# The output projection's weights in other parts, and one part in five transfers of unequal height

## Chip, cores and metric

One core of a Trainium2 chip runs the whole program. The metric is the device time of one execution in microseconds (us). The kernel before took 187.05 us, the median of three runs (187.05 to 187.24).

## What is computed

One decode step (a single new token for each of two batch rows) of a transformer block with adaptive layer norm: attention against a cache, then a gated FFN. Cut to what matters:

```python
mod = (silu(c) @ w_mod).reshape(2, 6, 1, -1)          # sa, ca, ga, sb, cb, gb
h = layernorm(x) * (1 + ca) + sa
q = (h @ wq) -> 32 heads of 192; k, v = the last 1024 rows of the caches
o = softmax(q k^T * 192**-0.5) v                       # per batch row and head
x = x + ga * (o.reshape(2, 1, 6144) @ wo)              # wo: 6144 x 640
h = layernorm(x) * (1 + cb) + sb
x = x + gb * ((gelu(h @ w_gate) * (h @ w_up)) @ w_down)
```

All inputs are bf16. With two rows of x, each weight and each cache row is read once and used little: the program moves some 77 MB for a few matmuls.

## The kernel before

The program is a list of operations per engine, written out in order. A helper class adds an operation or a DMA to its engine's list and derives from named buffers which semaphores it waits for. All DMAs are issued by SP in one order, through line 341, and so stand in one queue that 16 DMA engines work off.

That order is: w_mod, c, x, wq, four loads of K (two tiles each), five of V, then wo in parts, w_gate, w_up, and w_down in three parts, at the end the output. Two large areas of SBUF hold them: a ring of four tiles for K, V and at last the FFN's weights, and one area (`r1`) for wq, later K and V tiles, then wo (`wo_v`).

A load of a weight takes all 128 partitions: partition p gets rows p*n to p*n + n - 1 of the matrix, one contiguous stretch of memory. For wo that is 48 rows of 640 values per partition, and `WO_SPLIT` (line 227) cuts the 48 into parts that are loaded by a DMA each, with a semaphore each (`sem_wo`), lines 679 to 683. They wait for the last two uses of V of batch row 0 (`keep["pv", 0, 2]` and `keep["pv", 0, 3]`), whose area they overwrite. w_gate, w_up and w_down wait for the first uses of V of batch row 1.

```python
        for i, (ta, tb) in enumerate(wo_of):
            S.dma("sp", k_dma(wo_v[:, ta:tb, :].rearrange("p t n -> p (t n)"), wo_src[:, ta:tb, :].rearrange("p t n -> p (t n)")),
                  sem_wo[i], writes=[("wo", i)], deps=[keep["pv", 0, t] for t in (NTL - 2, NTL - 1)], name="ld_wo%d" % i)
```

Stages: the modulation and first layer norm, q (line 491), the scores as products on DVE (line 529) that PE sums (line 548), the softmax (from line 568), the weighted sum of V (lines 590 and 602), the output projection (line 706, one PE operation for each part of wo, which waits for that part), the second layer norm (line 716), the FFN (line 724 for w_gate and w_up, line 747 for w_down), and the two DVE operations and the store at the end (lines 754 to 758). Between the steps of the projection and of the FFN, PE runs matmuls whose results nobody reads (`warm`, line 521; how many is in `WO_WARM`, `WU_WARM`, `WD_WARM`).

Of the kernel before, what the change touches and what calls it, by code (L numbers as in the profile page):

```python
# [172 lines left out]
def bass_adaLN_cond__sliding_block_cached__geglu_ffn__decode_kernel(  # L173
# [15 lines left out]
    P = 128  # L189
# [18 lines left out]
    NTL = KP // J  # L208
# [15 lines left out]
    SL = J * Dh  # L224
    WQ_SPLIT = [5]
    assert sum(WQ_SPLIT) == KT
    WO_SPLIT = [16, 16, 12, 4]
    OT_SPLIT = [16, 16, 16]
    assert sum(WO_SPLIT) == NT and sum(OT_SPLIT) == NT
    WU_SPLIT = [5]  # L230
# [10 lines left out]
    with es:  # L241
        S = _Sched(nc, es)
# [6 lines left out]
        wo_v = r1.rearrange("p (t n) -> p t n", t=NT)  # L249
# [3 lines left out]
        def aux_f(a, n):  # L253
            assert a + n <= NAUX
            return aux[:, a:a + n]
# [18 lines left out]
        oT = aux_f(RN, NT * SQ).rearrange("p (t m) -> p t m", m=SQ)  # L274
# [48 lines left out]
        BK_M = 0  # L323
        SC = 256

        def bank(k):
            return ("bank", k)
# [4 lines left out]
        sem_wq = [S.sem("d_wq%d" % i) for i in range(len(WQ_SPLIT))]  # L332
        sem_wo = [S.sem("d_wo%d" % i) for i in range(len(WO_SPLIT))]
        sem_wg = S.sem("d_wg")
# [5 lines left out]
        def k_dma(dst, src):  # L340
            return lambda e: e.dma_start(dst, src)  # L341
# [5 lines left out]
        def dram_rows(v):  # L347
# [9 lines left out]
             reads=[("S", 0, 0, 0), ("S", 0, 0, 1), ("S", 0, 1, 0), ("S", 0, 1, 1)], writes=["ident_f"], name="ident_f")  # L357
        S.op("pool", lambda e: e.tensor_copy(out=ident_b[:, :], in_=ident_f[:, :]),
             reads=["ident_f"], writes=["ident_b"], name="ident_b")
# [3 lines left out]
             reads=["ident_f"], writes=["G32"], name="G32")  # L363
        S.op("dve", lambda e: e.tensor_reduce(out=M32[:, :], in_=ident_f[:, :].rearrange("p (h t) -> p h t", t=QP), axis=AX.X, op=ALU.add),
             reads=["ident_f"], writes=["M32"], name="M32")
# [3 lines left out]
             reads=["G32"], writes=["Bsel"], name="Bsel")  # L369
# [3 lines left out]
             reads=["M32"], writes=["DS"], name="DS")  # L373


        for b in range(2):
            S.op("dve", (lambda b: lambda e: e.tensor_copy(
                out=SEL[:, b, :, BS * b:P:SQ], in_=G32[:, :].rearrange("p (j m) -> p m j", m=HM)))(b),
                reads=["G32"], writes=["SEL"], name="SEL%d" % b)
        for b in range(2):  # L380
            for m in range(HM):
# [3 lines left out]
                    reads=["ident_f"], writes=["Qsel"], name="Qsel%d%d" % (b, m))  # L385
# [7 lines left out]
        keep = {}  # L393
# [14 lines left out]
        def slot_of(*it):  # L408
            return place[it]
# [75 lines left out]
        for i, (ka, kb) in enumerate(wq_of):  # L485
            def f(e, ka=ka, kb=kb):
                last = None
                for k in range(ka, kb):
                    for c in range(NQC):
                        for j in range(NJ):  # L490
                            last = e.matmul(ps[SQ * j:SQ * j + SQ, BK_H + c, 0:QC], lhsT=hT[:, k, :],  # L491
                                            rhs=wq_v[:, k, RN * j + QC * c:RN * j + QC * (c + 1)],
                                            start=(k == 0), stop=(k == KT - 1), tile_position=(0, SQ * j), skip_group_check=True)
                return last
# [22 lines left out]
        def warm(n, bk):  # L517
            def f(e):
                last = None
                for _ in range(n):  # L520
                    last = e.matmul(ps[:, bk, 0:2 * Dh], lhsT=ident_b[:, :], rhs=qbc[:, :, :].rearrange("p b d -> p (b d)"),  # L521
                                    start=True, stop=True)
                return last
            if n:
                S.op("pe", f, reads=["ident_b", "qbc"], writes=[bank(bk)], name="warm")
# [148 lines left out]
        for i, nt in enumerate(OT_SPLIT):  # L674
            S.op("dve", (lambda t0, nt: lambda e: e.transpose(oT[:, t0:t0 + nt, :], oc.rearrange("p (q k) -> p k q", k=NT)[:, t0:t0 + nt, :]))(t0, nt),  # L675
                 reads=[("oc", c) for c in range(NQC)], writes=[("oT", t) for t in range(t0, t0 + nt)], name="oT%d" % i)
            t0 += nt

        wo_src = A_wo.rearrange("(p t) n -> p t n", t=NT)
        wo_of = [(sum(WO_SPLIT[:i]), sum(WO_SPLIT[:i + 1])) for i in range(len(WO_SPLIT))]  # L680
        for i, (ta, tb) in enumerate(wo_of):
            S.dma("sp", k_dma(wo_v[:, ta:tb, :].rearrange("p t n -> p (t n)"), wo_src[:, ta:tb, :].rearrange("p t n -> p (t n)")),
                  sem_wo[i], writes=[("wo", i)], deps=[keep["pv", 0, t] for t in (NTL - 2, NTL - 1)], name="ld_wo%d" % i)
        assert slot_of("v", 1, 0) == 0 and slot_of("v", 1, 1) == 1
        r3_dead = [keep["pv", 1, 0], keep["pv", 1, 1]]
        S.dma("sp", k_dma(wg_v.rearrange("p k n -> p (k n)"), B_w_gate.rearrange("(p k) n -> p (k n)", k=KT)), sem_wg,
              writes=["wg"], deps=r3_dead, name="ld_wg")
# [13 lines left out]
        for i, (ta, tb) in enumerate(wo_of):  # L701
            def f(e, ta=ta, tb=tb):
                last = None
                for t in range(ta, tb):
                    for j in range(NJ):
                        last = e.matmul(ps[SQ * j:SQ * j + SQ, BK_M, 0:DN], lhsT=oT[:, t, :], rhs=wo_v[:, t, DN * j:DN * j + DN],  # L706
                                        start=(t == 0), stop=(t == NT - 1), tile_position=(0, SQ * j), skip_group_check=True)
                return last
            S.op("pe", f, reads=[("wo", i)] + [("oT", t) for t in range(ta, tb)], writes=[bank(BK_M)], name="wo%d" % i)
            warm(WO_WARM[i], 1)  # L710

        S.op("dve", lambda e: e.tensor_tensor(out=lnt[:, 0, :], in0=ps[:, BK_M, 0:DN], in1=modC[:, 2, :], op=ALU.mult),  # L712
             reads=[bank(BK_M), ("modC", 0)], writes=[("lnt", 0)], name="ga_attn")
        S.op("dve", lambda e: e.tensor_tensor(out=X2[:, 0, :], in0=lnt[:, 0, :], in1=X2[:, 0, :], op=ALU.add),
             reads=[("lnt", 0)], writes=[("X2", 0)], name="x1")
# [3 lines left out]
        def ffn_gu(bk, wv, key, name, ka, kb):  # L719
            def f(e):  # L720
# [11 lines left out]
             reads=[bank(BK_G[0])], writes=["gl"], name="gelu")  # L732
        k0 = 0
        for ci, nk in enumerate(WU_SPLIT):
# [4 lines left out]
             reads=[bank(BK_G[1]), "gl"], writes=["aC"], name="geglu")  # L739
        to_contraction(aT[:, :, :], aC[:, :], FT, ["aC"], ["aT"], "aT")  # L740
        f0 = 0
        for ci, nf in enumerate(WD_SPLIT):
            def f(e, f0=f0, nf=nf):
# [11 lines left out]
             reads=[bank(BK_C), ("modC", 1)], writes=[("lnt", 1)], name="gb_y")  # L755
        S.op("dve", lambda e: e.tensor_tensor(out=sc[:, :], in0=lnt[:, 1, :], in1=X2[:, 0, :], op=ALU.add),
             reads=[("lnt", 1), ("X2", 0)], writes=["sc"], name="outC")
# [36 lines left out]
```

## Time and profile before

| What | us |
|---|---|
| median of three runs | 187.05 |
| the profiled execution | 187.73 |
| its span, first to last instruction | 186.5 |
| busy: PE 117.4, DVE 106.6, ACT 13.9, POOL 4.9 | |
| DMA: 76.99 MB at 413 GB/s on the mean | |
| wo's four parts issued by SP | 138.42 to 140.18 |
| wo's parts landed | 156.83, 162.94, 168.22, 169.79 |
| w_gate, w_up landed | 174.37, 178.96 |
| w_down's three parts landed | 181.29, 182.82, 183.61 |

The profile counts from the start of the span. A DMA has landed when its semaphore has its last increment; the trace keeps the time of every increment and, for each packet on a DMA engine, its start, length and size, though not the engine's number. A 128-row load of wo appears as 128 packets of one row each and 16 packets of 4 bytes that raise the semaphore. PE is TensorE's matmuls, PEld its weight loads, DVE is VectorE, ACT ScalarE, POOL GpSimd, and SPq the DMA issues of SyncE.

### The profile page before, as it was taken

Reading aid. Unit: us, or ns where it says so; the run is one execution under the profiler, and the core shown is the slowest. Engines: PE = TensorE matmul, PEld = TensorE weight load, DVE = VectorE, ACT = ScalarE, POOL = GpSimd, SP = SyncE. Lnnn points to the kernel's source line nnn. Section 1 sums busy time; section 2 is a strip of 40 time slices with the busy share of each in tenths; the row PEclk is TensorE's granted clock in tenths of the full one; section 3 lists DMA queues with packets and bytes.
Section 4 is the critical chain, followed back from the end, with each engine's and each line's share of the span. In section 5 each row is a group of like instructions: output and inputs, shape, how many; then the busy total and the mean of one; then the engine's idle time right before and its main releaser. Section 6 shows DMA issues by size and latency. Waiting matters only on the chain.

```text
span 186.5 us, 2487 instructions
## 1 busy us (share of the span) xinstructions
PE 117.4 (63%) x1014; PEld 61.6 (33%) x1014; DVE 106.6 (57%) x114; ACT 13.9 (7%) x24; POOL 4.9 (3%) x12
## 2 busy tenths in 40 slices
PE   0004500860079998898988987329964998359854
PEld 0001200540034443444334443125642665236422
DVE  6801600020584999999999994454919453903431
ACT  2001400022000000000000000110010003200400
POOL 8100000000000000000000000000000000000000
PEclk9999999997557999999999999855998799996999
DMA  7999999899998989999998999999899999999980
GB/s 264 395 462 488 448 435 398 358 499 401 443 464 380 485 371 485 411 432 453 401 474 369 496 401 443 453 401 446 364 438 432 427 423 426 415 421 435 412 346 20
DMA packets 2923, 76.99 MB, mean 413 GB/s; under 512 B 356, under 2 KB 356, under 8 KB 868
## 3 DMA queue, kind: packets, MB, share of 16 engines
q1 hardware_dynamic: 2916, 76.88, 96.4%
q8 instruction: 6, 0.10, 0.2%
q14 instruction: 1, 0.01, 0.0%
HBM read 76.88 MB, written 0.00 MB: 412 GB/s over the span
## 4 chain that ended last, share of the span: by engine, by line
DMA 42%; DVE 36%; PE 17%; SPq 1%; ACT 1%; issue 1%; POOL 1%; DVEq 0%; POOLq 0%
DVE store L529 26%; DMA store<-in_A_k_cache_dram 24%; DMA store<-in_B_w_down_dram 17%; PE ps L602 11%; DVE Sg L562 5%; PE ps L548 4%; DVE Em L590 2%; SPq L341 1%; PE ps L541 1%; ACT E_sb L581 1%; PE ps L583 1%; PE ps L577 1%; DVE On L619 0%; ACT On L615 0%; PE ps L570 0%
## 5 line engine op out<-in xcount | busy, mean ns | idle before, releaser
L529 DVE TENSOR_TENSOR store<-store,qbc 128x6144 bf16<-128x6144 bf16 x16 | 53.5, 3347 | 8.8 <-DMA store<-in_A_k_cache_dram 8.8
L548 PE MATMUL ps<-store,ident_b 128*128 x192 | 46.5, 394 | 6.2 <-DVE store L529 6.2
L548 PEld LDWEIGHTS ps<-store,ident_b 128*128 128x128 bf16 x192 | 19.3, 100 | 31.4 <-issue 14.7
L602 PE MATMUL ps<-store,Em 128*64 128x384 bf16 x256 | 25.0, 364 | 6.6 <-DVE Em L590 6.6
L590 DVE TENSOR_TENSOR Em<-E_sb,M32b 128x2048 bf16<-128x2048 bf16 x8 | 18.1, 2288 | 5.9 <-PE ps L602 5.9
L602 PEld LDWEIGHTS ps<-store,Em 128*64 128x64 bf16 x256 | 15.7, 123 | 15.6 <-DVE Em L590 7.7
L541 PE MATMUL ps<-qbc,ident_b 128*128 128x384 bf16 x64 | 13.6, 338 | 10.9 <-DVE store L529 10.9
L468 PE MATMUL ps<-store,scT 128*32 128x480 bf16 x40 | 4.4, 601 | 15.8 <-DVE scT L425 15.8
L562 DVE TENSOR_REDUCE Sg<-ps 128x32 f32<-128x512 f32 x16 | 10.9, 683 | 5.7 <-PE ps L548 5.7
L491 PE MATMUL ps<-store,hT 128*32 128x384 bf16 x80 | 5.7, 470 | 10.7 <-DMA store<-in_A_wq_dram 10.7
L541 PEld LDWEIGHTS ps<-qbc,ident_b 128*128 128x128 bf16 x64 | 6.3, 100 | 17.0 <-issue 11.6
L501 DVE CAST aux<-ps 128x384 bf16<-128x384 f32 x4 | 2.0, 552 | 16.5 <-PE ps L491 15.6
L521 PE MATMUL ps<-qbc,ident_b 128*128 128x384 bf16 x56 | 11.0, 338 | 0.0
L706 PE MATMUL ps<-store,aux 128*32 128x160 bf16 x192 | 5.1, 269 | 5.2 <-issue 2.1
L491 PEld LDWEIGHTS ps<-store,hT 128*32 128x32 bf16 x80 | 3.2, 136 | 13.7 <-issue 11.6
L468 PEld LDWEIGHTS ps<-store,scT 128*32 128x32 bf16 x40 | 1.2, 132 | 17.3 <-DVE scT L425 15.8
L581 ACT ACTIVATE E_sb<-Sg,nb 128x256 bf16<-128x256 f32 x2 | 1.0, 508 | 78.0 <-DVE nb L580 78.0
L521 PEld LDWEIGHTS ps<-qbc,ident_b 128*128 128x128 bf16 x56 | 5.2, 101 | 3.8 <-issue 1.1
L706 PEld LDWEIGHTS ps<-store,aux 128*32 128x32 bf16 x192 | 4.2, 111 | 6.7 <-issue 4.4
L619 DVE TENSOR_SCALAR On<-ps,rden 32x192 bf16<-32x192 f32 x4 | 1.7, 418 | 7.6 <-ACT On L615 7.6
L712 DVE TENSOR_TENSOR lnt<-ps,modC 128x160 f32<-128x160 f32 x1 | 0.3, 325 | 7.8 <-PE ps L706 7.8
L675 DVE STREAM_TRANSPOSE aux<-aux 128x512 bf16<-128x512 bf16 x3 | 4.1, 1430 | 0.1
(70 smaller groups left out, 57.2 us busy)
## 6 DMA issues: line engine op xcount, KB each, us to landing
store<-in_A_k_cache_dram SPq DMA_DIRECT2D x4, 6144.0 KB, 39.7
store<-in_A_v_cache_dram SPq DMA_DIRECT2D x3, 6144.0 KB, 20.8
store<-in_A_wq_dram SPq DMA_DIRECT2D x1, 7680.0 KB, 30.5
store<-in_A_v_cache_dram SPq DMA_DIRECT2D x2, 3072.0 KB, 15.0
store<-in_A_wo_dram SPq DMA_DIRECT2D x2, 2560.0 KB, 21.3
store<-in_w_mod_dram SPq DMA_DIRECT2D x1, 4800.0 KB, 14.1
store<-in_A_wo_dram SPq DMA_DIRECT2D x1, 1920.0 KB, 28.9
store<-in_B_w_gate_dram SPq DMA_DIRECT2D x1, 1920.0 KB, 24.7
```

What stands on the lines that cost most here:

```text
L468: last = e.matmul(ps[SQ * j:SQ * j + SQ, bk, 0:3 * DN].rearrange("p (i n) -> p i n", i=3), lhsT=scT[:, k, :], rhs=wm_v[:, k, 3 * part * D: ...
L491: last = e.matmul(ps[SQ * j:SQ * j + SQ, BK_H + c, 0:QC], lhsT=hT[:, k, :], rhs=wq_v[:, k, RN * j + QC * c:RN * j + QC * (c + 1)], start=( ...
L521: last = e.matmul(ps[:, bk, 0:2 * Dh], lhsT=ident_b[:, :], rhs=qbc[:, :, :].rearrange("p b d -> p (b d)"), start=True, stop=True)
L529: S.op("dve", lambda e: e.tensor_tensor(out=tile_v(ks)[:, hf * JH:(hf + 1) * JH, :], in0=tile_v(ks)[:, hf * JH:(hf + 1) * JH, :], in1=qbc[ ...
L541: last = e.matmul(ps[:, BK_W, 0:2 * Dh], lhsT=ident_b[:, :], rhs=qbc[:, :, :].rearrange("p b d -> p (b d)"), start=True, stop=True)
L548: last = e.matmul(o_ap, lhsT=ident_b[:, :], rhs=tile[:, hf * JH:(hf + 1) * JH, ci * GC:(ci + 1) * GC], start=(ci == 0), stop=(ci == NCH - 1))
L562: S.op("dve", lambda e: e.tensor_reduce(out=S_sb[:, b, a:a + JH], in_=ps[:, hf, 0:JH * GC].rearrange("p (j c) -> p j c", j=JH), axis=AX.X, ...
L581: S.op("act", lambda e: e.activation(out=E_sb[:, b, :], in_=S_sb[:, b, :], func=ACTF.Exp, scale=SCALE, bias=nb[:, 0:1], accum_out=esum[:, ...
L590: S.op("dve", lambda e: e.tensor_tensor(out=Em[:, t % 2, :, :], in0=E_sb[:, b, J * t:J * (t + 1)].unsqueeze(2).broadcast_to([P, J, H]), in ...
L602: last = e.matmul(ps[r:r + 2 * H, BK_O, 0:ON], lhsT=Em[:, t % 2, 2 * jp:2 * jp + 2, :].rearrange("p j c -> p (j c)"), rhs=tile_v(vs)[:, 2 ...
L675: S.op("dve", (lambda t0, nt: lambda e: e.transpose(oT[:, t0:t0 + nt, :], oc.rearrange("p (q k) -> p k q", k=NT)[:, t0:t0 + nt, :]))(t0, n ...
L706: last = e.matmul(ps[SQ * j:SQ * j + SQ, BK_M, 0:DN], lhsT=oT[:, t, :], rhs=wo_v[:, t, DN * j:DN * j + DN], start=(t == 0), stop=(t == NT ...
```

## The change

wo's 48 rows per partition are cut 16, 16, 10, 6 instead of 16, 16, 12, 4. The third part goes out as five DMAs instead of one, one after another on SP: partitions 0 to 111, then 112 to 116, 117 to 121, 122 to 124 and 125 to 127. All five raise the semaphore of the third part, by 16 each, and the projection's third operation waits for all of them. What lands where in SBUF, the matmuls and their order stay the same, except that 40 of them instead of 48 belong to the third operation and 24 instead of 16 to the fourth.

```diff
-    WO_SPLIT = [16, 16, 12, 4]
+    WO_SPLIT = [16, 16, 10, 6]
+    UNEVEN = 2
+    EVEN_ROWS = 112
+    FEW = [5, 5, 3, 3]
+    assert EVEN_ROWS + sum(FEW) == P
...
+        wo_keys = []
         for i, (ta, tb) in enumerate(wo_of):
-            S.dma("sp", k_dma(wo_v[:, ta:tb, :].rearrange("p t n -> p (t n)"), wo_src[:, ta:tb, :].rearrange("p t n -> p (t n)")),
-                  sem_wo[i], writes=[("wo", i)], deps=[keep["pv", 0, t] for t in (NTL - 2, NTL - 1)], name="ld_wo%d" % i)
+            dst, src = wo_v[:, ta:tb, :].rearrange("p t n -> p (t n)"), wo_src[:, ta:tb, :].rearrange("p t n -> p (t n)")
+            pieces = [(dst, src)]
+            if i == UNEVEN:
+                pieces, p0 = [(dst[0:EVEN_ROWS, :], src[0:EVEN_ROWS, :])], EVEN_ROWS
+                for n in FEW:
+                    pieces.append((dst[p0:p0 + n, :], src[p0:p0 + n, :]))
+                    p0 += n
+            for k, (to, frm) in enumerate(pieces):
+                S.dma("sp", k_dma(to, frm), sem_wo[i], writes=[("wo", i, k)],
+                      deps=[keep["pv", 0, t] for t in (NTL - 2, NTL - 1)], name="ld_wo%d_%d" % (i, k))
+            wo_keys.append([("wo", i, k) for k in range(len(pieces))])
...
-            S.op("pe", f, reads=[("wo", i)] + [("oT", t) for t in range(ta, tb)], writes=[bank(BK_M)], name="wo%d" % i)
+            S.op("pe", f, reads=wo_keys[i] + [("oT", t) for t in range(ta, tb)], writes=[bank(BK_M)], name="wo%d" % i)
```

## The prediction

> **What bounds the kernel now.** I read the page's slices first, then the chain that ended last in order of time, then the end of the span in short stretches, and last the trace's records of single DMA packets. The page:
>
> ```profile
> span 186.5 us, 2487 instructions
> DMA  7999999899998989999998999999899999999980
> q1 hardware_dynamic: 2916, 76.88, 96.4%
> q8 instruction: 6, 0.10, 0.2%
> q14 instruction: 1, 0.01, 0.0%
> ```
>
> The 16 DMA engines are busy in every slice up to the last two, while no compute engine is. The second to last line shows six packets that fetch instructions on the same DMA engines; they matter below. The chain, in order of time (start, length, what):
>
> ```profile
> 151.47 32.13 DMA store<-in_B_w_down_dram
> 183.61 0.04 issue
> 183.65 0.35 PE ps L747 x8
> 184.00 0.02 issue
> 184.03 0.34 DVE lnt L754
> 184.37 0.02 issue
> 184.39 0.32 DVE sc L756
> ```
>
> The last piece of w_down was issued at 151.47, landed at 183.61, and 2.9 us of tail follow. So the end moves one for one with that landing, as long as PE is ready for it. Busy times by stretch (columns: window, length, busy time of PE, its weight loads, DVE, ACT, POOL, then clock, DMA share, GB/s):
>
> ```profile
> 178.00:180.00 2.00, 0.99 (x21) 0.51 (x22) 0.00 (x0) 0.00 (x0) 0.00 (x0) 1.00 1.00 406
> 180.50:181.00 0.50, 0.42 (x3) 0.03 (x1) 0.47 (x2) 0.00 (x0) 0.00 (x0) 1.00 0.74 292
> 181.00:181.50 0.50, 0.00 (x0) 0.00 (x0) 0.50 (x1) 0.00 (x0) 0.00 (x0) 1.00 0.44 179
> 182.00:182.50 0.50, 0.50 (x18) 0.24 (x8) 0.00 (x0) 0.00 (x0) 0.00 (x0) 1.00 0.22 87
> 183.00:183.50 0.50, 0.50 (x17) 0.26 (x16) 0.00 (x0) 0.00 (x0) 0.00 (x0) 1.00 0.01 5
> ```
>
> The share falls from 1.00 to 0.01 over 3 us: the 16 engines don't finish together. The packet records say why. On one DMA engine each packet starts within some ns of the end of the one before, and all run the same sequence of sizes (8 rows of every 128-row load, then a 4-byte packet), so the records chain into 16 sequences. Their last packets end at 180.40, 180.54, 180.56, 180.64, 180.74, 180.93, 181.00, 181.18, 181.20, 181.72, 182.13, 182.15, 182.17, 182.54, 182.66 and 183.18. The last six are the six whose sequence holds a 16,384-byte fetch (941 to 1102 ns, at 39.3, 130.1, 147.0, 163.9, 170.7 and 179.1 us); the one at 181.72 holds the 8,192-byte fetch at 66.7. A fetch sets its engine back by about 1.45 us against the median engine, for good. So one DMA engine bounds the kernel, 2.2 us behind the median one.
>
> **The change, part by part.** Prices first. Start to start on one engine, a row of 15,360 bytes takes 0.573 us, of 7,680 0.289, of 5,120 0.193. All lie on one line, 26.9 GB/s, so a row of the new third part (10 x 1,280 = 12,800 bytes) takes 0.289 + 5,120/7,680 x (0.573 - 0.289) = 0.478.
>
> Who gets which rows: 128-row loads raise their semaphore 16 times as they land, eight rows to an engine. The loads of c and x, whose outer size is 4, raise it four times, on the same four engines, those that end at 180.40, 180.93, 181.20 and 181.72. I take it that 112 rows go to 16 engines, seven each, and that 5 rows go to five and 3 rows to three engines of one fixed order, the four of c and x being its first. Call them engines 0 to 3; which is which the trace doesn't say, nor which engine is 4.
>
> Per engine, third and fourth part: before 8 x 0.573 + 8 x 0.193 = 6.13 us. After, engines 5 to 15: 7 x 0.478 + 8 x 0.289 = 5.66, a gain of 0.47. Engines 3 and 4 carry two rows more: + 0.49. Engines 0 to 2 carry four more: + 1.44, and four more 4-byte packets of some 13 ns, + 0.05. By this alone the last engine ends at 183.18 - 0.47 = 182.71, if engine 4 is none of the late ones and the one of 181.72 is engine 3 (181.20 + 1.49 = 182.69 for the latest of 0 to 2).
>
> What this leaves out is where the bytes go. The trace has no row for several DMA engines that write into neighbouring partitions at once. Bounds: nothing, if the pace of 26.9 GB/s is the engine's own; or, if it is that of the place written to, rows of one small transfer pass one behind the other. In full, all 16 rows in a file: 7.65 us instead of 4 x 0.478 = 1.91, + 5.74. One observation decides for me: the pace is the same in the full stream and for the last engine alone at 183 us (2,560 bytes in 99 ns both times), so it isn't shared bandwidth but something private, and in every load of 128 rows every engine has eight partitions to itself. The change is the first to break this pairing. An engine's own limit would look the same; I give the place 6 chances in 10. Sixteen places for 128 partitions hold eight each, so rows 112 to 119 and 120 to 127 lie behind two. The transfers of 5, 5, 3 and 3 rows then cost engines 0 to 2 at worst 5 + 3 + 3 + 3 = 14 rows of 0.478, 6.69, which is 4.78 over the free price. The four known engines reach the place up to 1.3 us apart (they ended that far apart), and engines that don't meet don't queue: I take half, 0.6, off. So engines 0 to 2 lose 1.44 + 4.78 - 0.6 = 5.6 us, from about 181.1 (the middle of the four) to 186.7: + 3.5 on 183.18. The place's usual engine shares it too and loses at most eight rows, 3.8 us, less its 0.47, hence no more than these. The seven rows per engine of the 112-row transfer might lose the pairing as well: nothing, or a doubling, 7 x 0.478 = 3.3; I take nothing, since each engine still has a run of its own.
>
> [...]
>
> Smaller edits. Four more issues on SP: 432 ns each by the wo rows, 547 to 716 by those of x and c, 1.7 to 2.9 us in all:
>
> ```profile
> 138.42 1.76 SPq L341 DMA_DIRECT2D store<-in_A_wo_dram  x4
> 149.67 0.33 SPq L341 DMA_DIRECT2D store<-in_B_w_gate_dram  x1
> ```
>
> Only wo's last part stands behind them; its first packet moves at 165. SP's next issue waits for PE until 149.67, so nine us are free and I cost this at nothing; without that cover, up to 2.9. PE waits once for wo part 2 as before, now for five landings. Its last wo step has 24 matmuls instead of 16: 64 take 1.29 us, so + 0.13 us on the way to the FFN. That is hidden by the wait for w_up:
>
> ```profile
> 179.00 1.00 PE L724 MATMUL ps<-store,hT 128*32 128x384 bf16 x20 [1.38 <-DMA store<-in_B_w_up_dram]
> 183.06 0.26 PEld L747 LDWEIGHTS ps<-store,aux 128*32 128x32 bf16 x16 [0.32 <-DMA store<-in_B_w_down_dram]
> ```
>
> In the slow case wo's last part lands on engines 0 to 2 at about 167.2 + 5.6 + 0.6 + 0.4 = 173.8 (median end of that part, loss, lag, landing) instead of 169.79, and the way to w_up's matmuls, 7 us of DVE and PE from there, ends near 181; w_up itself lands at 176.5 + 6.6 = 183.1. So DMA still ends last and the tail of 2.9 us stays.
>
> Sum: + 3.5 us. The profiled span is 186.5 inside an execution of 187.73; the median of the unprofiled runs is 187.05. I add the difference to that: 190.5, with 189.0 to 192.0 as the range of this case (loss 4.1 to 7.1 instead of 5.6).
>
> **Rivals.** First, the engine's own pace: writes to neighbours cost nothing, the last engine gains 0.47 us, PE follows (w_up lands 0.47 earlier, and PE's 0.32 us of idle before the w_down matmuls shows that it keeps up): 186.6. For it: the line through all row sizes needs no second limit. Against it: it needs both engine 4 and the one of 181.72 to be in the right place. Second, free writes but the wrong engines: with the one of 181.72 among engines 0 to 2 it ends at 181.72 + 1.49 = 183.21, no change, 187.1; with a late one as engine 4, the 183.18 one at worst, + 0.49, 187.5. [...]
>
> [...]
>
> **How the numbers follow.** Queue at the place 0.57, gain 0.25, about even 0.10, engine 4 late 0.04, one engine or a 112-row transfer that queues too 0.04. Some 0.2% (0.37 us) is what a measurement of this kernel can tell from no change. Faster is the gain case, 0.26 with a stray share of the even one; same 0.10; slower the rest, 0.64. The likeliest is slower: 190.5. The range runs from the gain, 186.5, to 192.2; what is left out is the queue beyond 5.1 us and the third rival.
>
> **What would show it.** Right: in the after trace wo part 2 lands over 2 us later than at 168.22, packets of 12,800 bytes on few engines take two to five times 0.478 us while the others keep pace, and three engines end last. Wrong: rows of 12,800 bytes keep 0.478 us everywhere, the DMA share falls to zero within 2.5 us instead of 3, and the last landing comes at 183.1. Were a fetch to hit one of engines 0 to 4 in the new program, 1.45 us would be added there, and the sum would fail in the gain case.

## The result and the profile after

The changed kernel takes 192.8 us, the median of six runs (192.56 to 193.29), against 187.05 (186.97 to 187.24): 1.031 times as long, 95% interval 1.0293 to 1.0327, or 5.75 us more. The forecast was 190.5, with 186.5 to 192.2 as the range: the right way, three fifths of the size, and the time lies 0.6 us outside.

The page of the changed kernel (a slice is 4.79 us):

```profile
span 191.6 us, 2491 instructions
DMA  7999998998999989989989999899999999999991
GB/s 248 417 554 410 423 410 369 482 465 359 482 400 431 474 359 482 472 349 492 451 369 472 441 400 472 369 475 400 405 426 451 417 410 346 213 195 427 426 380 41
q1 hardware_dynamic: 2932, 76.88, 96.7%
q8 instruction: 6, 0.10, 0.2%
q14 instruction: 1, 0.01, 0.0%
```

Slices 34 to 36, from 158 to 172 us, are where the time goes: 346, 213 and 195 GB/s, where the kernel before had more than 400. The row of DMA shares shows 9 all the same: the engines count as busy while they move half. Short stretches show it closer, first of the kernel before, then of the changed one (the last column is GB/s, the one ahead of it the DMA share):

```profile
161.00:165.00 4.00, 1.86 (x99) 1.51 (x88) 1.87 (x2) 0.00 (x0) 0.00 (x0) 1.00 0.99 416
165.00:169.00 4.00, 2.69 (x36) 1.59 (x39) 0.00 (x0) 0.00 (x0) 0.00 (x0) 0.81 1.03 430
169.00:172.00 3.00, 3.00 (x57) 2.02 (x49) 1.26 (x4) 0.00 (x0) 0.00 (x0) 0.69 1.01 422
```

```profile
161.00:165.00 4.00, 0.02 (x4) 0.03 (x8) 0.55 (x1) 0.00 (x0) 0.00 (x0) 0.56 1.00 215
165.00:169.00 4.00, 4.00 (x72) 2.94 (x72) 0.00 (x0) 0.00 (x0) 0.00 (x0) 0.58 1.00 197
169.00:172.00 3.00, 0.28 (x2) 0.00 (x0) 0.00 (x0) 0.00 (x0) 0.00 (x0) 0.96 0.92 176
174.00:178.00 4.00, 3.43 (x47) 1.80 (x36) 1.46 (x4) 0.00 (x0) 0.00 (x0) 0.50 1.01 428
```

In the 11 us from 161 to 172 the changed kernel moves 4 x 215 + 4 x 197 + 3 x 176 = 2,176 KB, which is 5.1 us of work at 428 GB/s: 5.9 us lost. The medians are 5.75 us apart and the two profiled executions 5.2, so the whole difference arises here. Before and after that stretch the pace is the old one: 451 GB/s from 155 to 160 us and 428 from 174 to 178, against 434 and 417. In the packet records the 128 rows of 12,800 bytes take 0.96 us at the median instead of 0.478, and so do rows that have nothing to do with the change: those of wo's second part that late engines still move (up to 1.54 us instead of 0.766), and most of its fourth part (0.56 to 0.99 instead of 0.291).

The chain that ended last is the old one, later by 5.16 us: w_down's last piece lands at 188.77 instead of 183.61, and 2.8 us of tail follow.

```profile
149.74 39.03 DMA store<-in_B_w_down_dram
188.77 0.04 issue
188.81 0.35 PE ps L761 x8
```

The extra issues on SP cost nothing, as forecast: eight for wo end at 139.68, and the next one is due at 147.92.

```profile
136.67 3.01 SPq L345 DMA_DIRECT2D store<-in_A_wo_dram  x8
147.92 0.35 SPq L345 DMA_DIRECT2D store<-in_B_w_gate_dram  x1
```

### The profile page after: what moved, and what is told of

Same layout as the page of the kernel before. It is cut to its first block, busy times and chain, and to the rows that moved or that the text cites. A ratio compares the mean times of both kernels' runs of the same rounds, so it can differ in the third digit from the quotient of the medians.

```text
span 191.6 us, 2491 instructions
## 1 busy us (share of the span) xinstructions
PE 118.2 (62%) x1014; PEld 63.1 (33%) x1014; DVE 106.6 (56%) x114; ACT 13.9 (7%) x24; POOL 4.9 (3%) x12
## 4 chain that ended last, share of the span: by engine, by line
DMA 44%; DVE 35%; PE 16%; SPq 1%; ACT 1%; issue 1%; POOL 1%; DVEq 0%; POOLq 0%
DVE store L533 26%; DMA store<-in_A_k_cache_dram 24%; DMA store<-in_B_w_down_dram 20%; PE ps L606 10%; DVE Sg L566 5%; PE ps L552 3%; DVE Em L594 2%; SPq L345 1%; PE ps L545 1%; ACT E_sb L585 1%; PE ps L587 1%; PE ps L581 1%; DVE On L623 0%; ACT On L619 0%; PE ps L574 0%
## 5 line engine op out<-in xcount | busy, mean ns | idle before, releaser
L552 PE MATMUL ps<-store,ident_b 128*128 x192 | 45.1, 386 | 6.2 <-DVE store L533 6.2
L606 PE MATMUL ps<-store,Em 128*64 128x384 bf16 x256 | 24.4, 356 | 6.9 <-DVE Em L594 6.6
L545 PE MATMUL ps<-qbc,ident_b 128*128 128x384 bf16 x64 | 13.7, 338 | 10.4 <-DVE store L533 10.4
L720 PE MATMUL ps<-store,aux 128*32 128x160 bf16 x192 | 6.2, 302 | 10.6 <-DMA store<-in_A_wo_dram 8.8
L525 PE MATMUL ps<-qbc,ident_b 128*128 128x384 bf16 x56 | 12.2, 367 | 0.0
L720 PEld LDWEIGHTS ps<-store,aux 128*32 128x32 bf16 x192 | 5.1, 125 | 12.0 <-DMA store<-in_A_wo_dram 9.8
```

The costliest lines, as they stand in the source:

```text
L545: last = e.matmul(ps[:, BK_W, 0:2 * Dh], lhsT=ident_b[:, :], rhs=qbc[:, :, :].rearrange("p b d -> p (b d)"), start=True, stop=True)
L552: last = e.matmul(o_ap, lhsT=ident_b[:, :], rhs=tile[:, hf * JH:(hf + 1) * JH, ci * GC:(ci + 1) * GC], start=(ci == 0), stop=(ci == NCH - 1))
L606: last = e.matmul(ps[r:r + 2 * H, BK_O, 0:ON], lhsT=Em[:, t % 2, 2 * jp:2 * jp + 2, :].rearrange("p j c -> p (j c)"), rhs=tile_v(vs)[:, 2 ...
```

## The experiments

Each ratio is to the kernel before on the same chip. A place is here, as in the prediction, a group of SBUF partitions that is supposed to take its writes one after another. Theory: a DMA engine's pace is that of the place in SBUF that it writes to; a load of 128 rows gives each engine a place to itself, other loads make engines meet. Rivals: the parts' sizes, the number of transfers, the few engines of a small transfer, or the addresses that are read.

### One part of the change alone

The split 16, 16, 10, 6, with each part in one transfer of 128 rows:

```diff
-    WO_SPLIT = [16, 16, 12, 4]
+    WO_SPLIT = [16, 16, 10, 6]
```

> wo in 16, 16, 10 and 6 parts, each part one transfer of 128 rows. If the loss of 5.75 us comes from transfers that are not of 128 rows, this stays at 187.05 us within 0.4, rows of 12,800 bytes take 0.478 us from start to start, and wo's part 2 lands near 167.3. If rows of 12,800 bytes are slow by themselves (rival), they take 0.95 us as in the changed kernel and the time is 187.05 + 8 x 0.478 = 190.9 us.

Measured: 187.01 us, ratio 0.9995 (0.9985 to 1.0005); the middle half of the rows of 12,800 bytes take 479 to 484 ns, and wo's third part (part 2) lands at 166.62 instead of near 167.3. The sizes are neutral, and the price of a row was right.

The same with the third part in five transfers that differ in columns, not in rows:

```diff
+            if i == 2:
+                pieces = [(dst[:, 2 * D * a:2 * D * (a + 1)], src[:, 2 * D * a:2 * D * (a + 1)]) for a in range(5)]
```

> The third part in five transfers too, but of 128 rows and two of the ten columns of parts each (2,560 bytes a row). Theory (only the pairing of engines and places counts): 40 rows of 0.099 instead of 8 of 0.478, 0.14 us more, and four more 4-byte packets, 0.05: 187.1 to 187.3 us. Rival (five transfers in place of one, their issues on SP and the joint wait of PE, cost part of the 5.75 us): 188 us or more.

Measured: 187.29 us, ratio 1.0013 (1.0004 to 1.0022). The number of transfers, their issues and PE's wait for five landings are not the cause either, although SP here ends its issues for w_down at 161.4 us instead of 151.9.

The 112 rows alone:

```diff
+            if i == 2:
+                pieces = [(dst[0:112, :], src[0:112, :])]
```

> The third part's transfer of 112 rows alone; rows 112 to 127 of that part aren't loaded (that much of wo is left out of the sum). Theory (its runs of seven rows don't keep engines and places paired): 7 x 0.478 = 3.3 us more, less 0.48 for the row that no engine carries: 189.9 us or somewhat above, and below 250 GB/s while it runs. As the prediction had it (each engine has a run of its own, free): 186.6 us.

Measured: 190.45 us, ratio 1.017 (1.0145 to 1.0195), 3.9 us above the 186.6 that this would take if it were free. Its stretches:

```profile
161.00:165.00 4.00, 0.40 (x16) 0.41 (x20) 1.19 (x1) 0.00 (x0) 0.00 (x0) 0.76 1.03 227
165.00:168.00 3.00, 1.81 (x60) 1.61 (x48) 0.00 (x0) 0.00 (x0) 0.00 (x0) 0.50 0.96 205
```

So the large transfer of 112 rows, seven to an engine, halves the pace by itself. The prediction had priced this at 3.3 us and then taken nothing.

The small transfers alone, on top of the kernel before:

```diff
+            if i == 3:
+                p0 = 112
+                for k, n in enumerate((5, 5, 3, 3)):
+                    few.append(S.dma("sp", k_dma(spare[p0:p0 + n, :], wo_src[p0:p0 + n, 32:42, :].rearrange("p t n -> p (t n)")),
...
+                    p0 += n
```

> wo's parts as before (16, 16, 12, 4, transfers of 128 rows); between the third and the fourth part four transfers of 5, 5, 3 and 3 rows of 12,800 bytes more, to partitions 112 to 127 of a spare tile, 205 KB that nothing uses. Theory of the place with the price of the prediction: engines 0 to 2 take 1.9 us for their four rows if free (end at 182.6 to 183.6, time 187.0 to 187.6), 6.7 - 0.6 = 6.1 us if they queue: 181.1 + 6.1 = 187.2, time near 191; the other engines' rows of wo's fourth part keep 0.193 us. Rival (small transfers slow all 16 engines): rows of the fourth part take twice as long or more on every engine while the small ones run.

Measured: 190.77 us, ratio 1.0193 (1.0177 to 1.0208). The time is the one the theory gave, but the rival's sign is there too: from 165.6 to 170.7 us rows of wo's fourth part take 0.28 to 0.55 us, whichever engine carries them, instead of 0.196. The loss isn't confined to the engines that carry them.

### Where the rows go

The next three keep the source rows of `few_alone`, or fewer of them, and change the partitions of the spare tile:

```diff
-                for k, n in enumerate((5, 5, 3, 3)):
-                    few.append(S.dma("sp", k_dma(spare[p0:p0 + n, :], wo_src[p0:p0 + n, 32:42, :].rearrange("p t n -> p (t n)")),
+                for k, (n, d0) in enumerate(((5, 0), (5, 1), (3, 2), (3, 3))):
+                    few.append(S.dma("sp", k_dma(spare[d0:d0 + 4 * n - 3:4, :], wo_src[p0:p0 + n, 32:42, :].rearrange("p t n -> p (t n)")),
```

> As few_alone, the same source rows and transfers of 5, 5, 3 and 3 rows, but they go to partitions 0, 4, 8, 12, 16 of the spare tile, then 1, 5, 9, 13, 17, then 2, 6, 10 and 3, 7, 11. Theory (the place in SBUF decides: engine n has partitions 4n to 4n+3 to itself in a load of 128 rows, so here every engine writes to its own place): rows keep 0.478 us, the other engines' rows keep their pace, 16 engines move 415 GB/s or more from 165 to 171 us, time 187.0 to 187.7. Rival (source addresses, or the mere number of engines in a transfer): 190.8 us as few_alone.

Measured: 187.25 us, ratio 1.0007 (0.9993 to 1.002). All 16 small rows take 479 to 486 ns. From 165 to 168 us:

```profile
165.00:168.00 3.00, 1.09 (x43) 0.70 (x45) 0.00 (x0) 0.00 (x0) 0.00 (x0) 1.00 1.03 427
```

For `few_alone` the same stretch has

```profile
165.00:168.00 3.00, 1.12 (x9) 0.66 (x9) 0.00 (x0) 0.00 (x0) 0.00 (x0) 0.94 1.08 255
```

Same bytes, same source rows, same number of engines: 427 against 255 GB/s. The partitions written to decide. It also shows that engines 0 to 4 had the time to spare that the change meant to use.

With the start partitions 64 to 67 instead of 0 to 3: by the theory a place each again, but one that another engine fills in a load of 128 rows:

> As few_own, to partitions 64, 68, 72, 76, 80 and so on: one engine to each place again, but a place that another engine fills in a load of 128 rows. Theory of the place: two streams meet at each, rows take 0.96 us on both sides, engines 0 to 2 end at 181.1 + 3.9 = 185.0, the usual owners at up to 183.2 + 1.9 = 185.1: about 189 us. Rival (only several engines of one small transfer queue among themselves): 187.0 to 187.7 us. Rival (source addresses): 190.8 us.

Measured: 189.26 us, ratio 1.0132 (1.0095 to 1.017), as the theory had it; most of the small rows take 0.9 to 0.99 us.

```profile
165.00:168.00 3.00, 1.86 (x10) 0.96 (x10) 0.00 (x0) 0.00 (x0) 0.00 (x0) 0.75 1.07 248
```

By the theory five places have two writers each, ten engines in all. If only these fell to half pace, all 16 together would keep 11/16 of 428 GB/s, 294. The packet records show that the other six are slow too: the 16 packets under way at 167.0 us are four small rows (0.90 to 0.93 us), eight rows of wo's fourth part (0.36 to 0.40 instead of 0.196) and four of w_gate (15,360 bytes, 1.09 to 1.12 instead of 0.573). Whether two writers at one place are enough for that was tested last, with four transfers of two rows to partitions 0 and 1, 2 and 3, 32 and 33, 34 and 35, so that two engines write side by side:

```diff
-                for k, n in enumerate((5, 5, 3, 3)):
+                for k, (n, d0) in enumerate(((2, 0), (2, 2), (2, 32), (2, 34))):
```

> [...] Theory (two writers at one place hold up all 16 engines, as in few_other where engines with nothing to share had half pace): 16 engines move under 320 GB/s for some 4 us from 165 on, rows of wo's fourth part take 0.3 us or more on most engines, 188 to 189 us. Rival (only engines that share a place are slow): 390 GB/s or more, fourth part's rows at 0.196 us on 14 engines, the time set by engines 0 and 1 alone, 181.1 + 3.8 = 184.9 at worst, 187.1 to 188.8 us.

Measured: 188.95 us, ratio 1.0094 (1.0065 to 1.0123).

```profile
165.00:168.00 3.00, 0.30 (x5) 0.21 (x5) 0.00 (x0) 0.00 (x0) 0.00 (x0) 1.00 1.02 389
```

The time lies in the theory's range and a little above the rival's 188.8, so it doesn't decide; the pace does, 389 GB/s next to the rival's 390. The two engines of the small transfers are slow (0.95 to 0.96 us a row once both are there, at partitions 32 to 35 as at 0 to 3), and 120 of the fourth part's 128 rows keep 0.21 us or less. The rival holds: two late engines set the time, for w_down's last piece lands at 182.99 or before on 14 engines and at 184.35 and 184.89 on two. So here two engines side by side cost only themselves, while in `few_other`, where by the theory ten meet, all 16 are slow.

### Other shapes of the third part

Transfers of 112 and 16 rows, of 64 and 64, and eight of 16 rows, with partitions in steps of eight or in a row:

```diff
+            if i == 2:
+                pieces = [(dst[a:P:8, :], src[a:P:8, :]) for a in range(8)]
```

> The third part in transfers of 112 and 16 rows, every one of the 16 engines with 7 + 1 rows. Theory (engines queue at the place in SBUF they write to, because a transfer that is not of 128 rows pairs engines and partitions otherwise): the 112 rows cost 7 x 0.478 = 3.3 us again, the 16 rows lie behind two places of eight partitions, 8 x 0.478 instead of 0.478, 3.3 more: about 193.7 us. Rival (the small transfers on few engines hold the others up): no transfer is on few engines, 187.1 us. Rival (the 112 rows alone are to blame): 190.4 us.

> The third part in two transfers of 64 rows, four rows to an engine in each. Theory of the place: 64 partitions in a row are half the places, 16 engines share them, every row takes 2 x 0.478: 8 x 0.478 = 3.8 us more, 190.9 us. Rival (only runs of an odd length, or few engines, are slow): 187.1 us, rows at 0.478 us.

> The third part in eight transfers of 16 rows, a row to each engine, partitions 0, 8, 16 to 120, then 1, 9, 17 and so on. If a place is eight partitions in a row, as the prediction had it, one engine writes to each: rows at 0.478 us, 187.1 us. [...]

> The third part in eight transfers of 16 rows to 16 partitions in a row. Places of eight in a row: 16 engines at two places, 7 x 3.8 = 27 us more, 214 us. [...]

| third part | us | ratio, 95% interval | GB/s from 161 to 165 |
|---|---|---|---|
| one transfer of 128 rows | 187.01 | 0.9985 to 1.0005 | 411 |
| 112 and 16 | 191.94 | 1.0247 to 1.0284 | 206 |
| 64 and 64 | 193.66 | 1.0344 to 1.0383 | 158 |
| 8 x 16, steps of eight | 192.01 | 1.0235 to 1.0281 | 195 |
| 8 x 16, in a row | 194.74 | 1.0380 to 1.0439 | 152 |

No transfer here is on few engines (the traces have 356 packets under 512 bytes in the kernel before, 372 with two transfers in place of one and 468 or 469 with eight, so each raises its semaphore by 16 packets of its own), so few engines aren't needed for a loss. Steps of eight were to be free if a place were eight partitions in a row; they cost 4.9 us, so the prediction's picture of the places was wrong. Which partitions share a place no run shows. Nor do the losses follow that picture's count of writers: 64 and 64 rows lose 6.6 us where two writers everywhere would lose 3.8, and 16 in a row 7.6 where it gave 27. The transfers of 112 and 16 rows came out between the theory's 193.7 and the 190.4 of the 112 rows alone. None of the four times that places of eight forecast, 193.7, 190.9, 187.1 and 214 us, came out right.

### A way to gain

In the kernel before, the six engines that end last, at 182.13 us and later, are those with a fetch of 16,384 bytes (0.94 to 1.10 us each), so a shorter program was tried, without 47 of PE's matmuls that nobody reads:

```diff
-    WO_WARM = [0, 8, 0, 9]
-    WU_WARM = [5]
-    WD_WARM = [5, 0, 0]
+    WO_WARM = [0, 0, 0, 0]
+    WU_WARM = [0]
+    WD_WARM = [0, 0, 0]
...
-        warm(12, 1)
...
-        warm(8, 1)
```

> The kernel before without the matmuls that nobody reads after the output projection began (47 of them, 94 instructions of PE, are left out). The bound is the DMA engine that instruction fetches set back most, 1.45 us each. Theory: a program with 94 instructions less fetches once less on the way to the end; if that fetch is one of those of the last engine, 185.6 to 186.6 us, if not, 187.05. Rival (PE's clock falls without them and PE ends last): 187.3 to 189 us.

Measured: 187.2 us, ratio 1.0005 (0.9991 to 1.0018). The theory fell: the trace still has six fetches of 16,384 bytes, and although the last, at 182.8 us, comes after the last row of the loads (182.47), w_down's last piece lands at 182.90, as in `split_alone` with all six ahead of the end. The rival's sign is there: the granted clock is 0.50 from 174 us on, and in the chain w_down's landing is no longer what ends last, PE is.

```profile
149.17 29.07 DMA store<-in_B_w_up_dram
178.28 1.82 PE ps L723 x16
181.69 1.82 PE ps L745 x44
183.53 0.34 DVE lnt L752
```

PE's last matmuls end at 183.51, in `split_alone` at 183.29, so the slower clock costs some 0.2 us here, too little to show in the ratio. No version that beats both kernels came out of this.

## Why the prediction was right or wrong

**The bound** was right: the landing of w_down's last piece sets the end before and after, and the difference is made in the DMA engines.

**The prices** of a row, of the split and of PE's wait held (`split_alone`, `cols5`). SP's four more issues took 1.25 us instead of 1.7 to 2.9 and were hidden, as forecast. The way rows are shared out held too: the small transfers raise their semaphore 16 times as they land (5 + 5 + 3 + 3), and `few_own`, where by the same sharing the n-th of these engines writes to partitions 4n to 4n + 3, was free: 187.25 us, rows at 479 to 486 ns. Two figures of the prediction are off without bearing on the sum: the last engine ends 2.0 us behind the median of the 16 ends that it lists, not 2.2, and eight matmuls more at 1.29 us for 64 are 0.16 us, not 0.13.

**Place or engine's own pace**, 6 chances to 4: place. `few_own` (187.25 us) against `few_alone` (190.77) and `few_other` (189.26) shows it. The sixteen places of eight partitions in a row that the sum rests on no run shows: rows in steps of eight, which would then be free, move at 195 GB/s instead of 411 (`r16_step8`). Engines that write closer together meet too: two within four partitions take 0.953 to 0.962 us a row instead of 0.478 (`few_pair`).

**The small transfers** were forecast at + 3.5 us in the sum and cost 3.7 alone. That the size fits is luck: I had three engines queue behind two places of eight partitions, while in `few_alone` all 16 engines fall to about half pace for some five microseconds (237 GB/s from 165 to 169 us, against 430). Of the signs that were named, wo's third part did land over 2 us later (172.85 instead of 168.22), but the slow rows are on all engines, not on few.

**The step that failed** is that of the 112 rows: "The seven rows per engine of the 112-row transfer might lose the pairing as well: nothing, or a doubling, 7 x 0.478 = 3.3; I take nothing, since each engine still has a run of its own." They lost it, and `r112_only` measures 3.9 us where the sum has nothing. The likely reason, my guess from `few_own` and not shown row by row: runs of seven cross the borders of the fours that were free there. The same step spoiled the range: with its own upper bound in the sum, 190.5 + 3.3 = 193.8, the range would have held the time, though 193.8 is 1.0 us too much.

**The sum** of the parts measured alone, 3.7 + 3.9 = 7.6, is more than the change's loss against its own free price, 192.8 - 186.6 = 6.2. Likely the two stretches overlap: alone, the 112 rows are slow from 161 to about 170 us and the small transfers from 165.5 to 171, so half pace would be paid once for both. No run took it apart.

**The gain rival**, 0.47 us, did not come about with these transfers, and the runs speak against it in general: a row taken off a late engine is written by another one to partitions that by the theory the late one fills too, and in `few_other`, which does the like, most such rows take 0.9 to 0.99 us instead of 0.478. No run tried it with a late engine's rows.

Open are which partitions share a place, how crowding at several places reaches engines with a place to themselves, and what sets the pace then (152 to 255 GB/s in the stretches above). That the reads play no part is shown for the small transfers alone; for the 112 rows the place is the likelier cause and was not separated from the order of the reads.

## What to carry to other kernels

Load through all 128 partitions, and cut a load by columns, not by rows, where its parts must be shorter: five transfers by columns cost 0.13%, one of 112 rows 1.7% (without the 16 rows that it leaves out). If a transfer has fewer rows, choose the partitions so that each engine writes where it writes in a full load: here that was worth 3.5 us (`few_own` at 187.25 us, `few_alone` at 190.77). A high share of busy DMA engines says nothing on their pace (1.00 at 215 GB/s, 1.01 at 428 in the changed kernel): read GB/s by stretch, and the lengths of packets of one size.

## What the runs showed that I had not expected

Two DMA engines that write side by side slow each other alone (`few_pair`: 389 GB/s in all, 120 of the fourth part's 128 rows at 0.21 us or less), but five that write where others do bring all 16 to about half pace (`few_other`: 248 GB/s). And a transfer of 112 rows, seven to each of 16 engines, loses about as much (3.9 us) as the small transfers on few engines (3.7).
